# Local-global attention with a gated feed-forward on one core: every second head from the 17th on has its exponentials transposed in blocks by VectorE and placed by DMAs, queries load in pairs, and the planner has new due offsets

## The chip, the cores and the metric

The kernel runs on one core of one Trainium2 chip. The metric is the device time of one execution in microseconds (us), the median of several executions. A core has five engines that run their own instruction lists side by side: TensorE (PE) for matrix products, VectorE (DVE), ScalarE (ACT), GpSimd (POOL), and SyncE (SP), which here only issues DMAs. They meet through semaphores. SBUF is the on-chip memory, PSUM the memory that PE writes its products to.

## What is computed

```python
def _attn_ref(q_l, k_l, v_l, q_g, k_g, v_g):      # 8 batches, 8 heads, 512 local + 32 global positions, 64 wide
    s_g = scale * np.matmul(q_g, k_all.transpose(0, 1, 3, 2))
    out_g = np.matmul(sm(s_g), v_all)
    s_ll = scale * np.matmul(q_l, k_l.transpose(0, 1, 3, 2))
    mask = np.abs(pos[:, None] - pos[None, :]) <= window          # window = 32
    s_ll = np.where(mask, s_ll, -1000000000.0)
    s_lg = scale * np.matmul(q_l, k_g.transpose(0, 1, 3, 2))
    a_l = sm(np.concatenate([s_lg, s_ll], axis=-1))
    out_l = np.matmul(a_l, np.concatenate([v_g, v_l], axis=2))
...
def _moe_ref(x, w1, w2, w3, w_out):                # 4352 tokens, 512 -> 1024 -> 512
    a = x @ w1
    b = x @ w2
    h = a * b @ w3
    return (h @ w_out).astype(np.float32)
```

`sm` is a softmax over the last axis. A local query sees the 32 global keys and the local keys at most 32 places away; a global query sees all 544 keys.

## The kernel before

**Heads.** There are 64 heads (8 batches of 8). For each head n the 512 queries are four blocks e of 128. `scores` multiplies a block with the 192 or 256 keys that it can see (with the 32 global ones), into PSUM tile `s`. `minus_max` (VectorE) adds the mask, takes the row's extreme and writes the shifted scores to the SBUF buffer `P`, of which there are two, for even and for odd heads. `exps` (ScalarE) takes the exponential in place and sums rows. The next product needs these weights with the keys on the partitions, so `transposes` lets PE transpose `P` through an identity matrix: seven 128x128 pieces into PSUM tiles `t` (lines 391 and 394). `weights_hi` and `weights_lo` split what comes out into a rounded half and a remainder (fp32r pairs, so that two fast products give fp32 accuracy), into the single buffers `PTh` and `PTl` (local keys) and `G` (global keys). Five pieces e = 0, 1, 2, 3, 6 of that split come from the transposed head, two (4, 5) from the global queries. `values` then makes the head's output `av`; `values_half`, `values_sum`, `join` and `normalize` bring it to tile `u`, and `convert` splits it into the feed-forward's input `x`.

**Feed-forward.** w3 and w_out are multiplied once into w34 (`fold`, 64 products, PE line 692). For each half batch (256 tokens, and once for the global tokens) there are four quarters: `first` makes `ap` and `bp` (48 products of 256 columns, lines 555 to 557), `gate_a`/`gate_b`/`gate_hi`/`gate_lo` multiply and split them, `second` adds them into `acc` (12 products of 512 columns, lines 585 to 587). The weights arrive packed in 64-bit words and are unpacked by VectorE and ScalarE (`unit`, lines 612 to 616) while the first heads run.

**Order.** Nothing is ordered at run time. `list_schedule` takes every step with its engines, its cost (`COST`, ns) and a due time, and emits each engine's instructions in a fixed order: at each moment an engine takes, among the steps that are ready, the one with the lowest due time. A PE step that has become ready less than 600 ns ago ranks 6.0 us later, once the plan is past 250 us (`MARGIN`, `LATE`, `MAIN`). The due time is a natural one (a head every 8 us, then every 11.2 us) plus offsets from the tables `DUE` (by kind of step and by stage: stage 0 to 2 reach to about head 14, stage 3 is all that follows), `HEADS`, `UNITS` and `SUMS`. All DMAs are issued by SP, also in that fixed order; one that waits holds all behind it. `take` sets how many buffers a tile has, and so which later step waits for which earlier one.

Of the kernel before, what the change touches and what calls it, by code (L numbers as in the profile page):

```python
# [20 lines left out]
KD = 608  # L21
WIN = [(0, 192), (96, 256), (256, 256), (416, 192)]
PAT = [0, 192, 448, 704]
PW = 896
# [6 lines left out]
def i(ap):  # L31
# [3 lines left out]
NX, NO, NK, MA = (5, 6), 3, 3, 4  # L35
# [8 lines left out]
    w12l=((691, 1300), (420, 752)), w34h=587, w34l=681, scores=897, transposes=690, values=560, gscores=505,  # L44
# [26 lines left out]
    av=(0, -8.3, -53.5, 0), cb=(0, -42.6, 22.6, 0), cg=(-24.3, 42.6, 2.5, 0), clear=(36.2, 0, 0, 0),  # L71
    eg=(11.2, -14.5, 60.9, 0), exps=(-77.6, 1.9, 61.5, 0), fetch=(-6.1, 67.6, -28.7, 0), first0=(0, 0, -0.5, 0),
    first1=(0, 0, 14.2, 0), fold=(0, 82.7, 0, 0), ga=(0, 0, 19.2, 0), gb=(0, 0, -4.6, 0), gh=(0, 0, -57.6, 0),
    gl=(0, 0, -25.9, 0), gw=(0, 35.2, 8.4, 0), hi0=(0, 9.7, -58.6, 0), hi1=(0, -25.8, -77.7, 0),
    hi2=(0, -54.5, -10.4, 0), hi3=(0, -77.2, -22, 0), hi4=(0, -21.9, 24.2, 0), hi5=(0, -3.2, -31.3, 0),
    hi6=(0, 14, 6.1, 0), inv=(-41, -86.6, -72.2, 0), invi=(-2.4, 7.2, -63.4, 0), invo=(-5.2, -59.2, 61.1, 0),
    join=(0, -72, 8.5, 0), joing=(0, 41.8, -10.6, 0), kh=(-29, -66.2, 23.9, 0), kl=(25, -37.7, 45.9, 0),
    kph=(-76.1, 18.5, 3.8, 0), kpl=(22.5, 58.7, 76.8, 0), lcs=(-13.6, 0, 0, 0), lk=(10.3, -26.8, -37.4, 0),
    lkp=(6.7, -0.4, 59.5, 0), lo0=(0, -27.3, -31.1, 0), lo1=(0, -41.7, -128.1, 0), lo2=(0, -80.3, -32.8, 0),
    lo3=(0, -22.1, -19.6, 0), lo4=(0, -11.9, 72.6, 0), lo5=(0, 15.6, 35.1, 0), lo6=(0, -109, -94.1, 0),  # L80
    lq=(9.1, -81.9, -50.8, 0), lqg=(34.3, 46.7, 4.5, 0), lv=(22.9, 41.7, 72.5, 0), lvg=(-24.1, 73.7, -106.8, 0),
    mg=(11.1, 4.8, 28.3, 0), mmax=(-67.6, -19.9, 10.3, 0), mul=(0, 2.8, -12.7, 0), ng=(-9.8, -40.4, 19.2, 0),
    out=(0, 0, 31.5, 0), qgh=(-9.8, 6, 147.2, 0), qgl=(36.9, -10.2, 1.5, 0), qh=(54.2, -4.8, 102.4, 0),
    ql=(-40, 112.7, 18.6, 0), s=(173.8, 31.8, -49.9, 0), second=(0, 0, -11.5, 0), sg=(-103.1, 12.4, -39.4, 0),
    store=(0, 0, 68.3, 0), sum=(0, -31.9, 18.7, 0), t=(0, -40.4, -94.3, 0), tg=(0, -106.1, 15.3, 0),
# [17 lines left out]
}  # L103
SUMS = (-30.2, -40.9, -14, 28.4, 21.4, -13.3, 36.6, 38.3)
# [81 lines left out]
def band_attention_glu_kernel(  # L186
# [91 lines left out]
    def load_vg(b):  # L278
        vgr = p2.tile([64, 512], F32, tag="qr", name=f"vgr{b}", bufs=3)
# [36 lines left out]
    def prep_q(n, part, eng=None):  # L316
        if part == 0:
            T["qs", n] = p1.tile([128, 512], F32R, tag="qs", name=f"qs{n}")
            hi_of(T["qs", n][0:64], T["qr", n], eng)
        else:  # L320
            qs = T["qs", n]
            lo_of(qs[64:128], T.pop(("qr", n)), qs[0:64], eng)
# [827 lines left out]
```

## Time and profile before

| | |
|---|---|
| median of 3 runs | 900.78 us (899.81 to 900.85) |
| span of the profiled execution, first to last instruction | 896.8 us |
| what lies around the span, against the median | 4.0 us |
| VectorE busy | 631.9 us |
| ScalarE busy | 631.4 us |
| GpSimd busy | 424.1 us |
| DMA traffic | 87.06 MB |

The profile shows one execution. Its page names for each engine the busy time; a chain of waits that is followed back from the last instruction, which tells what the end hung on; groups of equal instructions with the mean duration of one; and DMA issues with the time until they have landed. The trace behind it answers for stretches of the span (windows) and as a list in order of time. Matrix products overlap each other in PE's pipeline: a listed duration of 0.28 us does not mean that the next one starts 0.28 us later. What one costs PE is the distance from start to start.

### The profile page before, as it was taken

To read this page: it belongs to the slowest core of one execution; us is meant where nothing else is said; L and a number is where in the kernel's file an instruction comes from. 1 tells how busy PE (TensorE), PEld (TensorE's weight loads), DVE (VectorE), ACT (ScalarE), POOL (GpSimd) and SP (SyncE) were. 2 spreads that over 40 slices of the span, in tenths; PEclk is the share of its full clock that TensorE was granted. 3 is DMA by queue.
4 is the path that set the end of the run, shared out by engine and by line. 5 is a ranking of instruction groups with operands and counts; after the bars stand their busy time and mean duration, and the time that the engine had idled before them with its cause. 6 is when DMAs were issued, how large, how long until landed. Compare 5 with 4: busy or idle time off the path is not lost.

```text
span 896.8 us, 17972 instructions
## 1 busy us (share of the span) xinstructions
PE 844.0 (94%) x6016; PEld 766.0 (85%) x6016; DVE 631.9 (70%) x1644; ACT 631.4 (70%) x1724; POOL 424.1 (47%) x492
## 2 busy tenths in 40 slices
PE   3879969799999999999999999999999999999995
PEld 2545549699899999999999999999999999999994
DVE  4998988778877778777777777777777787512111
ACT  5887887787878787878787878787877777512111
POOL 4454765655655555555555455555555545200000
PEclk9999989999999999999999999999999999999998
DMA  9877545332242423232323332323232311000000
GB/s 273 246 219 215 181 149 139 118 98 83 65 118 69 111 63 115 61 106 68 113 67 106 77 101 80 101 68 114 65 107 65 108 57 48 13 24 24 1 24 24
DMA packets 52853, 87.06 MB, mean 97 GB/s; under 512 B 16024, under 2 KB 17048, under 8 KB 52760
## 3 DMA queue, kind: packets, MB, share of 16 engines
q1 hardware_dynamic: 52760, 85.92, 33.1%
q8 instruction: 47, 0.77, 0.4%
q14 instruction: 46, 0.38, 0.2%
HBM read 76.84 MB, written 9.04 MB: 96 GB/s over the span
## 4 chain that ended last, share of the span: by engine, by line
PE 87%; DVE 4%; ACT 4%; DMA 2%; issue 1%; POOL 1%; SPq 1%; DVEq 0%; ACTq 0%; POOLq 0%
PE ap L555 7%; PE acc L585 7%; PE acc L587 7%; PE bp L555 7%; PE ap L556 7%; PE acc L586 7%; PE ap L557 7%; PE bp L556 7%; PE bp L557 7%; PE s L355 6%; PE av L446 6%; PE w L692 4%; PE t L391 3%; PE t L394 2%; PE av L441 2%; PE sg L482 2%
## 5 line engine op out<-in xcount | busy, mean ns | idle before, releaser
L555 PE MATMUL bp<-x,w12h 128*128 128x256 f32 x544 | 154.8, 285 | 0.8 <-DVE g__1696 L565 0.8
L555 PE MATMUL ap<-x,w12h 128*128 128x256 f32 x544 | 153.7, 283 | 0.0
L556 PE MATMUL ap<-x,w12h 128*128 128x256 f32 x544 | 152.1, 280 | 0.0
L557 PE MATMUL ap<-x,w12l 128*128 128x256 f32 x544 | 151.6, 279 | 0.0
L556 PE MATMUL bp<-x,w12h 128*128 128x256 f32 x544 | 151.2, 278 | 0.0
L557 PE MATMUL bp<-x,w12l 128*128 128x256 f32 x544 | 151.1, 278 | 0.0
L289 POOL TENSOR_TENSOR kl<-kr,kh 128x608 fp32r<-128x608 f32 x62 | 93.5, 1508 | 104.8 <-ACT kh L286 102.0
L363 ACT ACTIVATE P<-P,mn 128x192 f32<-128x192 f32 (+1 forms) x256 | 121.5, 477 | 5.5 <-DVE mn L359 4.8
L460 DVE TENSOR_TENSOR u<-av,cb 64x352 f32<-64x352 f32 x128 | 65.8, 521 | 58.5 <-ACT cb L286 55.8
L555 PEld LDWEIGHTS bp<-x,w12h 128*128 128x128 f32 x544 | 102.5, 188 | 1.9 <-DVE g__1696 L565 0.9
L556 PEld LDWEIGHTS ap<-x,w12h 128*128 128x128 f32 x544 | 103.6, 190 | 0.5
L555 PEld LDWEIGHTS ap<-x,w12h 128*128 128x128 f32 x544 | 103.5, 190 | 0.5
L556 PEld LDWEIGHTS bp<-x,w12h 128*128 128x128 f32 x544 | 102.5, 188 | 1.1
L557 PEld LDWEIGHTS ap<-x,w12l 128*128 128x128 f32 x544 | 103.4, 190 | 0.0
L557 PEld LDWEIGHTS bp<-x,w12l 128*128 128x128 f32 x544 | 102.4, 188 | 0.0
L359 DVE CUSTOM_DVE_ANT_0 P<-s,cs 128x192 f32<-128x192 f32 (+1 forms) x256 | 87.3, 387 | 7.7 <-PE s L355 5.6
L289 DVE TENSOR_TENSOR PTl<-t,PTh 32x96 fp32r<-32x96 f32 (+1 forms) x192 | 76.3, 397 | 19.2 <-ACT PTh L286 14.3
L286 ACT CAST PTh<-t 32x96 fp32r<-32x96 f32 (+1 forms) x190 | 66.5, 350 | 22.9 <-PE t L391 15.5
L286 ACT COPY cb<-av 64x352 f32<-64x352 f32 x128 | 57.0, 446 | 32.4 <-PE av L446 29.3
L355 PE MATMUL s<-kh,qs 128*128 128x192 f32 (+1 forms) x256 | 65.9, 292 | 8.5 <-DVE mg L497 3.3
L692 PE MATMUL w<-wo,w3f 128*128 128x512 f32 x128 | 63.8, 635 | 3.9 <-DVE wo L616 3.8
L446 PE MATMUL av<-PTl,vs 128*128 128x192 f32 (+1 forms) x256 | 64.5, 277 | 0.0
(786 smaller groups left out, 2350.8 us busy)
## 6 DMA issues: line engine op xcount, KB each, us to landing
kr<-in_kd_t_dram SPq DMA_DIRECT2D x128, 152.0 KB, 2.9
raw_w<-in_w_t_dram SPq DMA_DIRECT2D x24, 512.0 KB, 4.3
kpr<-in_kp_t_dram SPq DMA_DIRECT2D x32, 272.0 KB, 2.7
out_dram<-o SPq DMA_DIRECT2D x34, 256.0 KB, 2.2
qr<-in_q_t_dram SPq DMA_DIRECT2D x64, 128.0 KB, 2.7
vr<-in_v_t_dram SPq DMA_DIRECT2D x32, 256.0 KB, 2.7
R<-rd SPq DMA_DIRECT2D x64, 128.0 KB, 3.0
raw_wo<-in_wo_t_dram SPq DMA_DIRECT2D x8, 512.0 KB, 6.4
```

What stands on the lines that cost most here:

```text
L286: (nc.scalar.copy if eng in (None, nc.scalar) else eng.tensor_copy)(dst, src)
L289: (eng or nc.gpsimd).tensor_sub(dst, src, f(hi))
L355: nc.tensor.matmul(st[:, e, 0:w], qs[:, 128 * e : 128 * e + 128], kk[:, o : o + w], start=(j == e % 2 == 0), stop=(j == 1), skip_group_che ...
L359: nc.vector.tensor_tensor_reduce(blk(n, e), T["st", n][:, e, 0 : WIN[e][1]], masks[e], -0.125, 3.0e38, ALU.add, ALU.min, T["mn", n][:, e : ...
L363: nc.scalar.activation(blk(n, e), blk(n, e), AF.Exp, bias=T["mn", n][:, e : e + 1], scale=-1.0, accum_out=T["sm", n][:, e : e + 1])
L446: nc.tensor.matmul(av[:, o : o + c1 - c0], v, pt[:, j, c0:c1], start=False, stop=(j % 2 == y == 1), skip_group_check=True)
L460: nc.vector.tensor_add(T["u", n // 2][r : r + 64, x], T.pop(("av", n, x))[r : r + 64, 0:352], T["cb", n][r : r + 64, x])
L555: nc.tensor.matmul(d, wh[:, k, c, :], x[:, 0, 0:w], start=(k == m % 2 == 0), stop=False, skip_group_check=True)
L556: nc.tensor.matmul(d, wh[:, k, c, :], x[:, 1, 0:w], start=False, stop=False, skip_group_check=True)
L557: nc.tensor.matmul(d, wl[:, k, c, :], x[:, 0, 0:w], start=False, stop=(k == 3), skip_group_check=True)
L585: nc.tensor.matmul(a, gh[:, m % 2, sl], wh, start=(m == 0), stop=False)
L692: nc.tensor.matmul(T["w34", t], T["w3f", t, j // 4][:, j % 4], T["wo"][:, j], start=(j == 0), stop=(j == 7))
```

## The change

From head 17 on, every odd head ("turned", 24 heads) is no longer transposed by PE. `minus_max` writes its shifted scores to another layout of `P` (1120 instead of 896 columns): eight slots of four blocks e of 32 columns. `turn` lets VectorE transpose 32x32 blocks in place with three instructions (5 slots = 640 columns, 2 slots = 256, 32 columns). A 32x32 transpose leaves each block at its old place in the partitions, so DMAs move the blocks: `turned_out` writes five slots to a DRAM buffer `pd` with four DMAs (rows of 512 bytes) and copies two pieces of 32x96 from partition group to partition group; `turned_in` reads `pd` back into `P` in the new arrangement with two DMAs. The split into halves then reads `P` in SBUF instead of `t` in PSUM, in four pieces instead of five, and its remainders (`lo`) may run on GpSimd as well as on VectorE. These heads have their scores due 6 us earlier (`AHEAD`). The queries of two heads load with one DMA of 128 partitions; the split of an odd head's query works on the upper half. GpSimd clears a spare part of both `P` once. The four tables of offsets are new throughout: those of before lie within about 185 us of zero, and those of stage 3 were all zero; the new ones reach to 2900 us, in stage 3 too.

```diff
-PW = 896
+PW = 1120
+TURN, FROM, AHEAD = 2, 16, 6.0
+def turned(n):
+    return n >= FROM and n % TURN == TURN - 1
...
-    av=(0, -8.3, -53.5, 0), cb=(0, -42.6, 22.6, 0), cg=(-24.3, 42.6, 2.5, 0), clear=(36.2, 0, 0, 0),
+    T=(0, 0, 0, -189.6), av=(0, -2661.5, -798.8, -1384), av_=(0, 0, 0, -1664), cb=(0, -875.8, -862.7, -832.2),
...
-    def load_q(n):
-        b, h = divmod(n, H)
-        qr = p2.tile([64, 512], F32, tag="qr", name=f"qr{n}", bufs=3)
-        nc.sync.dma_start(qr, q_t[b, h])
+    def load_q(m):
+        b, p = divmod(m, NP)
+        qr = p2.tile([128, 512], F32, tag="qr", name=f"qr{m}", bufs=NQ)
+        nc.sync.dma_start(qr, q_t[b, 2 * p : 2 * p + 2].rearrange("h d s -> (h d) s"))
...
+    def turn(n):
+        g = grid(n)
+        nc.vector.transpose(g[:, 1:6], g[:, 1:6])
+        nc.vector.transpose(g[:, 0:8:7], g[:, 0:8:7])
+        nc.vector.transpose(g[:, 1, 0], g[:, 6, 0])
+
+    def turned_out(n):
+        P = Ps[n % 2]
+        d = T["pd", n] = dram.tile([5, 32, 4, 128], F32, tag="pd", name=f"pd{n}", bufs=2)
+        for x in range(4):
+            nc.sync.dma_start(d[:, :, x].rearrange("s p w -> p s w"),
+                              P[32 * x : 32 * x + 32, 128:768].rearrange("p (s w) -> p s w", s=5))
+        nc.sync.dma_start(P[96:128, 32:128], P[0:32, 32:128])
+        nc.sync.dma_start(P[0:32, 1024:1120], P[96:128, 896:992])
+
+    def turned_in(n):
+        P = Ps[n % 2]
+        d = T.pop(("pd", n))
+        nc.sync.dma_start(P[:, 256:768], d[1:5].rearrange("s p x w -> (s p) (x w)"))
+        nc.sync.dma_start(spread(n, [256]), d[0].rearrange("p (a b) w -> p a (b w)", b=2))
...
+        if turned(n):
+            t -= 4.0 + AHEAD
+            take("pd", 2, ("pd", n), ("dw", n))
+            add(("T", n), only("DVE", COST["turn"]), t, [("exps", n, e) for e in range(4)], turn, n)
+            add(("dw", n), dma(6), t + 1.0, [("T", n)], turned_out, n, nbytes=360448)
+            add(("dr", n), dma(2), t + 2.0, [("dw", n)], turned_in, n, nbytes=327680)
```

What this makes of the instruction lists is seen at head 39, in the middle of the program. **PE** before, where the products `bp` of a quarter end, head 39 is transposed (`t_39`) and head 40's scores `s` begin:

```order
L555 MATMUL bp_1_4_6646<-x_3_1_5532,w12h_1472 128x256
L556 MATMUL bp_1_4_6646<-x_3_1_5532,w12h_1472 128x256
L557 MATMUL bp_1_4_6646<-x_3_1_5532,w12l_1473 128x256
L391 MATMUL t_39_6737<-cs,P_74 128x128 x4
L394 MATMUL t_39_6738<-cs,P_74 128x128 x3
L355 MATMUL s_6748<-kh_6634,qs_6639 128x192
L355 MATMUL s_6748<-kl_6662,qs_6639 128x192
```

and PE now, at the same place:

```order
L627 MATMUL bp_1_4_6672<-x_3_1_5588,w12h_1192 128x256
L628 MATMUL bp_1_4_6672<-x_3_1_5588,w12h_1192 128x256
L629 MATMUL bp_1_4_6672<-x_3_1_5588,w12l_1193 128x256
L395 MATMUL s_6692<-kh_6563,qs_6609 128x192
L395 MATMUL s_6692<-kl_6583,qs_6609 128x192
```

The seven transposes are gone, and the scores follow the feed-forward directly; over the program PE has 280 of these transposes instead of 448, and all its other products are as many as before. **VectorE** now, at head 39 (`P_74`): three block transposes, then the inverse of its row sums (`sm`) and work of head 38 (`u`) and of the feed-forward (`gl`):

```order
L429 STREAM_TRANSPOSE P_74<-P_74 128x640
L430 STREAM_TRANSPOSE P_74<-P_74 128x2x128
L431 STREAM_TRANSPOSE P_74<-P_74 128x32
L408 TENSOR_SCALAR sm_6525<-sm_6525 128x4
L409 RECIPROCAL sm_6525<-sm_6525 128x4
L532 TENSOR_TENSOR u_6645<-av_38_6615,cb_6634 64x352
L532 TENSOR_TENSOR u_6645<-av_38_6621,cb_6634 64x352
L311 TENSOR_TENSOR gl__6668<-g__6607,gh__6664 128x512
```

The first remainder of head 39 (`PTl<-P_74`) stands 20 rows further on, behind a gate, a global softmax and the four `minus_max` of head 40. Before, the remainders (`PTl<-t_39`, `G<-t_39`) were read from PSUM and there was no such gap. **SP** now, with the same head's DMAs (`pd` is the DRAM buffer, `rd` and `R` carry its row sums, `kr` and `qr` are loads of later heads):

```order
L279 DMA kr_6604<-in_kd_t_dram 64x608
L280 DMA kr_6604<-in_kd_t_dram 64x608
L437 DMA pd_6627<-P_74 32x5x128 x4
L439 DMA P_74<-P_74 32x96
L440 DMA P_74<-P_74 32x96
L414 DMA rd_6670<-sm_6525 128x4
L445 DMA P_74<-pd_6627 128x512
L446 DMA P_74<-pd_6627 32x2x256
L420 DMA R_6559<-rd_6670 64x512
L273 DMA qr_6738<-in_q_t_dram 128x512
```

Eight DMAs are new in a turned head; the last two wait until the first six have landed, and the loads behind them wait as well.

More of the change, by code (lines that the diff above doesn't have):

```diff
@@ L43 @@
     gl=(691, 1295), out=587, shift=(434, 295), scale=(680, 440), merge=(676, 424), w12h=(676, 423),
-    w12l=((691, 1300), (420, 752)), w34h=587, w34l=681, scores=897, transposes=690, values=560, gscores=505,
+    w12l=((691, 1300), (420, 752)), w34h=587, w34l=681, scores=897, turn=1260, turned=((620, 512, 691, 1295), (290, 96, 257, 290), (290, 96, 257, 290), (620, 512, 691, 1295)),
+    transposes=690, values=560, gscores=505,
     gtrans=465, first=1440, second=1405, fold=900,
@@ L76 @@
[L76 to L85, printed above, removed]
@@ L318, in prep_q @@
             T["qs", n] = p1.tile([128, 512], F32R, tag="qs", name=f"qs{n}")
[L319 to L322 removed]
+        qs, r = T["qs", n], 64 * (n % 2)
+        qr = T["qr", n // 2][r : r + 64]
+        if part == 0:
+            hi_of(qs[r : r + 64], qr, eng)
+        else:
+            lo_of(qs[64 - r : 128 - r], qr, qs[r : r + 64], eng)
     def prep_v(n, s, part, eng=None):
@@ L340, in prep_kp, with grid, spread, cut @@
             lo_of(T["kpl", m], T.pop(("kpr", m)), T["kph", m], eng)
+    def grid(n):
+        return Ps[n % 2][:, 0:1024].rearrange("p (s e q) -> p s e q", e=4, q=32)
+    def spread(n, dims):
+        P = Ps[n % 2]
+        steps = [1]
+        for w in dims[:0:-1]:
+            steps.insert(0, steps[0] * w)
+        return bass.AP(P.tensor, P.offset, [[PW, 32], [768, 2], *([x, w] for x, w in zip(steps, dims))])
+    def cut(n, ap):
+        return ap.rearrange("p (s q) -> p s q", q=32) if turned(n) else ap
     def blk(n, e):
-        return Ps[n % 2][:, PAT[e] : PAT[e] + WIN[e][1]]
+        if not turned(n):
+            return Ps[n % 2][:, PAT[e] : PAT[e] + WIN[e][1]]
+        s = 0 if e else 2
+        return grid(n)[:, s : s + WIN[e][1] // 32, e]
     def scores(n):
@@ L719, in moved @@
             kind += str(key[2])
+        if k in BY_HEAD and turned(key[1]):
+            kind += "_"
         d = DUE.get(kind, (0, 0, 0, 0))[stage]
@@ L768, in tile_orders @@
             take("kr", NK, (*k, "r"), ("load", *k))
-        for k in (("q", 0), ("q", 1), ("vg", 0)):
-            take("qr", 3, (*k, "r"), ("load", *k))
+        take("qr", NQ, ("q", 0, "r"), ("load", "q", 0))
+        take("kr", NK, ("vg", 0, "r"), ("load", "vg", 0))
         for k in (("sg", 0), ("s", 0), ("sg", 1), ("tg", 0)):
@@ L777, in tile_orders @@
                 take("kr", NK, ("k", n + 2, "r"), ("load", "k", n + 2))
-                take("qr", 3, ("q", n + 2, "r"), ("load", "q", n + 2))
+                if n % 2 == 0:
+                    take("qr", NQ, ("q", n // 2 + 1, "r"), ("load", "q", n // 2 + 1))
                 if (n + 2) % H == 0:
-                    take("qr", 3, ("vg", (n + 2) // H, "r"), ("load", "vg", (n + 2) // H))
-            for x in range(2):
+                    take("kr", NK, ("vg", (n + 2) // H, "r"), ("load", "vg", (n + 2) // H))
+            for x in range(2 * (not turned(n))):
                 take(f"t{x}", 1, (f"t{x}", n), ("t", n))
@@ L849, in head @@
             me = ("av", n, x)
-            add(me, only("PE", COST["values"]), t + 4.2 + 0.1 * x, [("lo", n, e) for e in range(7)] + v + [("av", n, 0)] * x, values, n, x)
+            add(me, only("PE", COST["values"]), t + 4.2 + 0.1 * x, [("lo", n, e) for e in parts] + v + [("av", n, 0)] * x, values, n, x)
             tiles["vs", n // 2].append(me)
@@ L1051, in band_attention_glu_kernel @@
     add(("load", "cs"), dma(1), -40.0, (), constants, nbytes=294912)
-    for x, (ap, ns) in enumerate(((QG, 525), (PTh, 957), (PTl, 962), (G[64:128], 552), (vgs[64:128], 952))):
-        k = ("QG", 0, 1, 2, "vgs")[x]
-        add(("clear", k), only("POOL", ns), (-60.0, -4.0, -4.0, -4.0, -4.0)[x], (), clear, ap)
+    spare = [p[:, 896:1024] for p in Ps]
+    for x, (ap, ns) in enumerate(((QG, 525), (PTh, 957), (PTl, 962), (G[64:128], 552), (vgs[64:128], 952), *((s, 200) for s in spare))):
+        k = ("QG", 0, 1, 2, "vgs", "P0", "P1")[x]
+        add(("clear", k), only("POOL", ns), (-60.0, -4.0, -4.0, -4.0, -4.0, -4.0, -4.0)[x], (), clear, ap)
     for n, u in enumerate(ORDER):
```

100 lines of the change are left out of this document (76 added, 24 removed), and 21 rows, old and new, of the table UNITS.

## The prediction

> **What bounds the kernel now.** I read the page's first lines and its chain of waits, then the windows, then PE's list in order of time.
>
> ```profile
> span 896.8 us, 17972 instructions
> PE 844.0 (94%) x6016; PEld 766.0 (85%) x6016; DVE 631.9 (70%) x1644; ACT 631.4 (70%) x1724; POOL 424.1 (47%) x492
> PE 87%; DVE 4%; ACT 4%; DMA 2%; issue 1%; POOL 1%; SPq 1%; DVEq 0%; ACTq 0%; POOLq 0%
> ```
>
> PE is busy for 94% of the span and carries 87% of the chain that sets the end. That is an average over stages, so the windows come next. Columns: stretch, its length, busy us (instructions) of PE, weight loads, VectorE, ScalarE, GpSimd, then granted clock, DMA share, GB/s.
>
> ```profile
> 0.00:40.00 40.00, 22.40 (x82) 14.14 (x82) 26.20 (x71) 26.90 (x67) 20.09 (x25) 0.96 0.88 257
> 40.00:80.00 40.00, 33.78 (x133) 19.34 (x134) 37.30 (x87) 32.14 (x88) 17.44 (x22) 0.96 0.80 227
> 80.00:160.00 80.00, 68.35 (x369) 50.72 (x368) 68.86 (x165) 65.44 (x174) 54.11 (x66) 0.94 0.54 162
> 200.00:300.00 100.00, 98.59 (x751) 93.56 (x751) 78.35 (x209) 78.76 (x221) 52.71 (x60) 1.00 0.31 89
> 408.71:500.56 91.85, 91.85 (x708) 87.50 (x708) 71.52 (x195) 73.12 (x205) 48.57 (x55) 1.00 0.31 88
> 760.00:880.00 120.00, 120.00 (x884) 113.14 (x884) 33.02 (x65) 29.10 (x66) 11.61 (x16) 1.00 0.05 16
> ```
>
> Three stages. In the ramp PE has gaps while VectorE (37.3 of 40) and ScalarE unpack weights. From about 200 us PE is full: the row from 408.71 to 500.56 is one period of eight heads, PE 100%, VectorE 78%, ScalarE 80%, DMA 31%. From 770 us only feed-forward is left, PE still full. So from 200 us on a microsecond less for PE is a microsecond less at the end, as long as nobody keeps PE waiting. The turned heads 17 to 63 lie almost wholly there.
>
> **What the change takes from PE.** The listed durations overlap, so I go by starts.
>
> ```profile
> 511.32 0.60 PE L391 MATMUL t<-cs,P 128*128 128x128 f32 x4
> 511.76 0.49 PE L394 MATMUL t<-cs,P 128*128 128x128 f32 x3
> 512.01 0.33 PE L355 MATMUL s<-kh,qs 128*128 128x192 f32 x1
> 512.98 0.30 PE L555 MATMUL ap<-x,w12h 128*128 128x256 f32 x1
> 515.74 0.28 PE L555 MATMUL bp<-x,w12h 128*128 128x256 f32 x1
> 517.68 0.40 PE L585 MATMUL acc<-w34h,gh__6974 128*128 128x512 f32 x1
> 519.07 0.28 PE L441 MATMUL av<-G,vgs 128*128 128x256 f32 x1
> ```
>
> The seven transposes hold PE from 511.32 to 512.01, **0.69 us** (by their listed mean of 278 ns it would be 1.95). 24 heads x 0.69 = **16.6 us** off PE. Its other products stay the same in number.
>
> **What it adds, and what hides it.**
>
> ```profile
> L289 DVE TENSOR_TENSOR PTl<-t,PTh 128x512 fp32r<-128x512 f32 x64 | 43.9, 687 | 8.5 <-ACT PTh L286 7.3
> L289 DVE TENSOR_TENSOR G<-t,G 32x384 fp32r<-32x384 f32 x64 | 35.8, 560 | 1.0
> L289 DVE TENSOR_TENSOR PTl<-t,PTh 32x96 fp32r<-32x96 f32 x128 | 32.3, 253 | 10.7 <-ACT PTh L286 7.0 <-ACT G L286 0.5
> L289 DVE TENSOR_TENSOR G<-t,G 32x128 fp32r<-32x128 f32 x64 | 17.9, 280 | 1.5 <-ACT G L286 0.5
> L289 DVE TENSOR_TENSOR qs<-qr,qs 64x512 fp32r<-64x512 f32 x23 | 27.4, 1189 | 1.6 <-ACT qs L286 0.8
> L289 POOL TENSOR_TENSOR qs<-qr,qs 64x512 fp32r<-64x512 f32 x41 | 55.7, 1359 | 13.4 <-ACT qs L286 6.4 <-issue 2.4 <-POOL kl L289 1.1
> L510 DVE TENSOR_SCALAR Pg<-Pg,smg 128x544 f32<-128x544 f32 x16 | 9.4, 584 | 0.6
> L612 DVE TENSOR_SCALAR raw_w12s<-raw_w12s 128x256 int32<-128x256 int32 x16 | 8.4, 529 | 1.7 <-DMA raw_w12s<-in_w_t_dram 1.6
> ```
>
> No row shows a block transpose. By the nearest one (584 ns for 544 columns) the 928 columns of three instructions cost 1.0 us; by the slowest near one (529 ns for 256) 1.9. I take 1.1, nearer the float row: 24 x 1.1 = 26 us for VectorE. [...] It loses the remainders from PSUM: 0.687 + 0.560 + 2 x 0.253 + 0.280 = 2.03 us a head, 48.8 in all. In the new order it does 29 large and 19 small remainders from SBUF: 19 x 0.253 plus 29 times between 0.687 and 1.189 (the row with two SBUF inputs), so 25 to 39 us. And 21 of the query remainders go to GpSimd: 25 us off VectorE, 28 onto GpSimd, which has half its time free. VectorE ends between +2 and -23 us: its cover at 78% stays. ScalarE's rounding reads as many elements as before.
>
> [...]
>
> **The new wait.** A turned head's weights now go through DRAM, and this chain must fit between its scores and its values on PE.
>
> ```profile
> L363 ACT ACTIVATE P<-P,mn 128x256 f32<-128x256 f32 x128 | 64.0, 502 | 0.2
> L363 ACT ACTIVATE P<-P,mn 128x192 f32<-128x192 f32 x128 | 57.9, 452 | 5.3 <-DVE mn L359 4.8
> L363 ACT ACTIVATION_READ_ACCUMULATOR P<-P,mn 128x1 f32 x256 | 48.4, 189 | 0.0
> L359 DVE CUSTOM_DVE_ANT_0 P<-s,cs 128x192 f32<-128x192 f32 x128 | 45.3, 354 | 6.9 <-PE s L355 5.6
> L286 ACT CAST PTh<-t 128x512 fp32r<-128x512 f32 x64 | 37.5, 586 | 16.1 <-PE t L391 15.5
> L286 ACT CAST PTh<-t 32x96 fp32r<-32x96 f32 x126 | 29.0, 230 | 6.8 <-PE t L394 4.1
> out_dram<-o SPq DMA_DIRECT2D x34, 256.0 KB, 2.2
> R<-rd SPq DMA_DIRECT2D x64, 128.0 KB, 3.0
> rd<-sm SPq DMA_DIRECT2D x64, 2.0 KB, 2.0
> q1 hardware_dynamic: 52760, 85.92, 33.1%
> 517.36 0.47 SPq L257 DMA_DIRECT2D kr<-in_kd_t_dram  x1
> 517.88 0.59 SPq L258 DMA_DIRECT2D kr<-in_kd_t_dram  x1
> ```
>
> First `minus_max` 0.35; four exponentials with their sums 2 x 0.691 + 2 x 0.641 = 2.66; block transposes 1.1; six writes, five issues at 0.47 to 0.59 and then 2.0 to 2.2 to land, 4.9; two reads, one issue and 3.0 to land, 3.5; rounding two large and two small pieces 1.63 and a last remainder, 2.1; handovers about 0.7, my estimate. Sum **15.3 us**. At worst: transposes 1.9, a last remainder under contention +0.5, and the write bound by its 704 packets: 0.331 x 16 x 896.8 / 52760 = 90 ns each, 704 / 16 x 0.09 = 4.0, with landing 6.2. Sum 17.9.
>
> The room for it: between head 39's scores and its values PE's order has 72 first products at (515.74 - 512.98) / 24 = 0.115, 24 second ones at (519.07 - 517.68) / 6 = 0.232, 16 scores at 0.121, 5 transposes at 0.099 and 14 others at about 0.115: **17.9 us**. The same count gives 19.6, 19.3 and 19.6 at heads 41, 43 and 45, and the pattern repeats every eight heads. So 2.6 us are spare at one turned head in four and 4 or more at three, for queueing on engines that are 80% busy. Behind the waiting reads SP holds `R`, `qr` and a key load; behind the waiting rounding ScalarE holds exponentials of the next head and a gate's rounding, for which PE's `t` and `acc` wait. I count the wait as hidden, with small slips:
>
> - **Slips, +4.** From head 15 on the new offsets are hundreds to thousands of us, so the planner's 6 us against steps that are only just ready no longer decides, and attention goes first the moment it is ready in the plan; any lateness then reaches PE. Before, that was so only early: in 200 to 300 us PE lost 1.41 of 100, later nothing. Over some 560 us that bounds it at 8; below it is 0. I take half.
> - **Ramp, +3.** Ahead of the first gate VectorE's order has eight more pieces of small w12 weights, each with a shift (529 ns) and a merge of about as much: 8 us more where it is 93% busy. But the big w12 pieces come earlier in ScalarE's order. Bounds -10 and +10.
> - **Tail, -1.4.** See the last gate:
>
> ```profile
> 882.33 0.70 DVE g__11784 L565
> 883.06 0.63 ACT gh__11786 L286
> 883.73 0.50 PE acc L585
> ```
>
> PE has 1.4 us of `acc` (six products) left to fill this gate of 1.4 us and its waits; the new order keeps twice as much for it. At most 1.4, at least 0.
>
> The 24 x 0.68 MB of new traffic come on a DMA share of 0.31; eight new issues of about 0.5 a turned head lie beside 22 us. The paired query loads save 32 issues that nobody waited for: 0.
>
> **Sum.** 896.8 - 16.6 + 4 + 3 - 1.4 = 885.8 us of span. Around the span lie 4.0 us (896.8 against the median of 900.8), so **889.8 us**.
>
> **The rivals.**
> - *The gain is kept whole and the ramp shortens.* No slips, ramp -7: 900.8 - 16.6 - 1.4 - 7 = 876; with the ramp unchanged 883. Middle 880. For it: PE has 35 us of gaps in the first 160. Against: VectorE limits there, and gets no lighter. 12%.
> - *The trip through DRAM is late at the tight heads only.* 1.3 us late (the packet bound) at six heads: 889.8 + 7.8 = 897.6. 10%.
> - *Given back in the new order.* Slips at 8, ramp at 10: 900.8 - 16.6 - 1.4 + 18 = 900.8. That is also where "PE is not the bound after all" would end. 10%.
> - *The trip through DRAM takes over as the bound.* Queueing eats the spare time, and write and transposes are at their bounds, 1.3 + 0.8 = 2.1 us late. Six heads lose 2.1, eighteen with 1.3 more room 0.8: 27 us. 900.8 - 16.6 + 27 - 1.4 + 3 = 912.8. It is slower from a lateness of 1.6 us on: 6 x 1.6 + 18 x 0.3 = 15, the net gain. [...] Against: both bounds at once, and no spare at all. 16%.
>
> That PE keeps its transposes is excluded by the order.
>
> **Chances and range.** Forecast 889.8 (884 to 895): 52%. Faster is forecast, whole gain and tight heads: 74%. Within 0.2%, about what a measurement of this kernel can tell from no change: 10%. Slower: 16%. The range of 879 to 903 takes in the forecast, the two middle rivals and most of the fastest, and leaves out the slowest.
>
> **What would show it.** PE at 100% in a period of eight heads that is 2.8 us shorter than 91.85; block transposes near 1.1 us together; `pd` landing within 5 us of its first issue; no waits of `av` or `acc` on ScalarE, GpSimd or DMA beyond 200 us; first full PE stretch again near 200 us. Wrong would be: PE waits at every turned head's `av`, VectorE over 90%, or a granted clock under 1.00 there.

## The result, and the profile after

| | before | after |
|---|---|---|
| median (runs) | 900.82 us (899.53 to 903.29, 6) | 895.14 us (893.53 to 898.31, 6) |
| profiled execution: span | 896.8 us | 896.5 us |
| ratio of times, 95% interval | | 0.9944 (0.9923 to 0.9964) |

The kernel became faster by 5.7 us by the medians (5.0 by the ratio, which is taken over all runs): inside the range, but at most about half of the forecast 11.0. The profiled execution was the slowest of its six (898.31 us), so its span hardly differs from before; a second profile of the same kernel (`again`, below) was of one that took 892.58 us. In every execution of this result and of the experiments the time is only 1.7 to 2.0 us longer than the span of the same execution. So the 4.0 us that were read as lying around the span before are in part something else: the profiled execution of before was a fast one, of about 898.6 us by this estimate (896.8 + 1.8). The forecast difference of 11.0 does not depend on that, and the two spans 896.8 and 890.8 compare about 898.6 with 892.58 us. The page's first lines after the change:

```profile
span 896.5 us, 17912 instructions
PE 832.8 (93%) x5848; PEld 753.6 (84%) x5848; DVE 630.3 (70%) x1623; ACT 616.4 (69%) x1671; POOL 491.2 (55%) x592
```

The windows after the change (stretch, length, busy us of PE, weight loads, VectorE, ScalarE, GpSimd, granted clock, DMA share, GB/s):

```profile
0.00:40.00 40.00, 19.13 (x61) 11.90 (x62) 24.33 (x63) 22.96 (x53) 15.70 (x22) 1.00 0.84 260
40.00:80.00 40.00, 35.79 (x139) 20.15 (x138) 34.38 (x83) 32.04 (x82) 15.54 (x22) 0.96 0.79 227
80.00:160.00 80.00, 58.98 (x251) 41.75 (x249) 64.21 (x159) 62.48 (x169) 51.03 (x59) 0.81 0.50 153
160.00:200.00 40.00, 39.54 (x306) 37.81 (x307) 35.72 (x92) 33.79 (x95) 26.47 (x33) 1.00 0.34 97
200.00:300.00 100.00, 97.26 (x740) 91.88 (x739) 78.48 (x222) 78.93 (x226) 64.65 (x77) 1.00 0.42 113
400.00:500.00 100.00, 99.17 (x751) 93.88 (x750) 77.04 (x208) 77.07 (x215) 65.84 (x78) 1.00 0.46 119
500.00:600.00 100.00, 98.20 (x742) 92.89 (x741) 75.21 (x208) 76.31 (x213) 66.84 (x78) 1.00 0.45 119
700.00:760.00 60.00, 58.01 (x444) 54.99 (x443) 48.78 (x125) 44.77 (x131) 34.01 (x44) 1.00 0.35 91
```

Two things stand out. PE is no longer full everywhere beyond 200 us. And the stretch 80 to 160 us, where PE was busy for 68.35 us at a clock of 0.94, now has 58.98 at 0.81; PE is full from 160 us instead of 200, which returns 5.6 of these 9.4 us. This row is of before:

```profile
160.00:200.00 40.00, 33.94 (x235) 31.83 (x234) 29.50 (x82) 30.84 (x89) 25.33 (x32) 0.91 0.33 103
```

The dip sits in 30 us; the first row is of before, the second of after:

```profile
120.00:150.00 30.00, 21.29 (x147) 20.38 (x148) 24.90 (x62) 24.93 (x71) 20.36 (x23) 0.83 0.45 125
```

```profile
120.00:150.00 30.00, 13.47 (x62) 11.50 (x61) 24.42 (x64) 24.50 (x69) 17.78 (x22) 0.67 0.46 132
```

The rows also say what is missing there. Before, the first product of the feed-forward (`ap`) starts at 132.5 us, and 86 of the 147 products between 120 and 150 us are `ap` and `bp`. After, the first one starts at 151.4 us (150.3 in `again`), so that in the dip PE has only attention, whose products wait for other engines.

**What PE lost, as one number.** Busy time can't be compared between clocks (up to 200 us a product of 256 columns takes PE 0.213 us where the records show the clock at 0.5, and 0.114 at 1.00), so I sum for each profile what every distance between the starts of two neighbouring matmuls has beyond the median distance behind a matmul of that line and shape. That counts gaps and half clock alike. "Head" is the start of the first matmul plus the sum up to 200 us, "main" the sum from 200 to 760, "tail" what follows. (The expectations below give the loss before 200 us without the start of the first matmul, so their figures are 9 to 11 us lower.)

| profile | span | head | main | tail | ideal PE work |
|---|---|---|---|---|---|
| before | 896.8 | 61.5 | 5.0 | 1.0 | 819.2 |
| after | 896.5 | 70.1 | 15.4 | 0.2 | 800.8 |
| after, again | 890.8 | 69.0 | 10.8 | -0.1 | 801.0 |

The last column is the sum of the median distances: what they make of the span without any loss. What starts with the last matmul takes 10.2 us more, the same in all three. With it, ideal + head + main + tail is the span to about 0.1 us, so the loss can be placed: from before to `again` it is -18.2 + 7.5 + 5.8 - 1.1 = -6.0. Some two fifths of the gain are lost in the head. Of the 7.5 us there, 5.3 are idle time of PE, as the first 200 us show (before, then `again`: 41.5 us idle, then 46.8); the other 2.2 are products that follow each other more slowly.

```profile
0.00:200.00 200.00, 158.47 (x815) 116.03 (x816) 161.87 (x402) 155.32 (x414) 116.97 (x143) 0.94 0.62 182
0.00:200.00 200.00, 153.21 (x763) 111.64 (x764) 158.95 (x395) 151.85 (x396) 110.25 (x134) 0.90 0.60 178
```

**Where the main part loses.** PE's waits between 200 and 800 us (engine, line, what it waited for, us in total, times, longest), first the only one of before, then the longest of the profile after:

```profile
PE s L355 <- DVE TGg L527: 1.3, 1, 1.3
```

```profile
PE sg L554 <- DVE mn L399: 3.7, 3, 2.0
PE ap L627 <- ACT as__2970 L633: 1.1, 1, 1.1
PE s L395 <- ACT TGg L599: 0.9, 1, 0.9
PE av L518 <- DVE PTl L311: 0.9, 1, 0.9
PE av L513 <- DVE G L311: 0.6, 1, 0.6
```

The longest wait is not at `av`, which uses the turned weights, but at `sg`, the global scores. The chain of waits shows how (start, us, what):

```profile
698.73 0.38 SPq L414
...
699.27 0.32 SPq L445
699.59 0.05 issue
699.65 7.03 DMA P<-pd
...
706.76 0.62 ACT PTh L308
...
708.02 0.42 DVE P L399
...
708.78 0.77 PE sg L554 x4
```

The read-back (L445), which SP issues behind the row sums' write (L414), takes 7.03 us here; only then does ScalarE round `PTh` out of `P` and VectorE take the remainder. This is head 57. What waits behind it is `minus_max` (L399) of head 58, an even head, which writes the other `P`. VectorE's list shows why:

```profile
702.19 0.41 DVE L399 CUSTOM_DVE_ANT_0 P<-s,cs 128x256 f32<-128x256 f32 x1
702.53 0.07 DVE L399 DVE_READ_ACCUMULATOR2_ANT mn<- 128x1 f32 x1
707.41 0.69 DVE L311 TENSOR_TENSOR PTl<-P,PTh 128x512 fp32r<-128x512 f32 x1 [4.80 <-ACT PTh L308]
708.02 0.42 DVE L399 CUSTOM_DVE_ANT_0 P<-s,cs 128x256 f32<-128x256 f32 x1
```

Two of head 58's four `minus_max` are done at 702.6 us; head 57's remainder comes next in VectorE's fixed order, waits for 4.80 us, and the other two stand behind it. `minus_max` is what empties PSUM tile `s`, and the global scores `sg` take turns with it in that one buffer. So here a late trip reaches PE through VectorE's list, and not through the values. Heads 25, 33, 41 and 49 have the same order, the remainder between the second and the third `minus_max` of the next head, and PE's three waits at `sg` stand behind heads 33, 41 and 57. At head 39, which was looked at before, the remainder stands behind all four.

ScalarE's own wait and the DMAs' medians:

```profile
ACT PTh L308 <- DMA P<-pd: 24.6, 17, 3.5
```

```profile
pd<-P SPq DMA_DIRECT2D x96, 80.0 KB, 1.9
P<-pd SPq DMA_DIRECT2D x24, 256.0 KB, 4.5
P<-pd SPq DMA_DIRECT2D x24, 64.0 KB, 4.4
```

The trip is late for ScalarE at 17 of 24 heads. The writes do as forecast (from the end of the block transposes to the last landing 4.4 us in the median, for a forecast of 4.9), the reads do not: 4.5 us instead of 3.0.

### The profile page after: what moved, and what is told of

Read it like the earlier page. It is cut to its first block, busy times and chain, and to the rows that moved or that the text cites. A ratio compares the mean times of both kernels' runs of the same rounds, so it can differ in the third digit from the quotient of the medians.

```text
span 896.5 us, 17912 instructions
## 1 busy us (share of the span) xinstructions
PE 832.8 (93%) x5848; PEld 753.6 (84%) x5848; DVE 630.3 (70%) x1623; ACT 616.4 (69%) x1671; POOL 491.2 (55%) x592
## 3 DMA queue, kind: packets, MB, share of 16 engines
q1 hardware_dynamic: 76824, 102.24, 40.8%
## 5 line engine op out<-in xcount | busy, mean ns | idle before, releaser
L311 POOL TENSOR_TENSOR qs<-qr,qs 64x512 fp32r<-64x512 f32 x62 | 82.2, 1325 | 83.1 <-ACT qs L308 68.7
L627 PEld LDWEIGHTS ap<-x,w12h 128*128 128x128 f32 x544 | 102.5, 188 | 4.1 <-ACT as__2970 L633 1.5
L628 PEld LDWEIGHTS ap<-x,w12h 128*128 128x128 f32 x544 | 102.3, 188 | 1.3 <-POOL x L311 0.2
L399 DVE CUSTOM_DVE_ANT_0 P<-s,cs 128x192 f32<-128x192 f32 (+1 forms) x256 | 86.9, 387 | 13.1 <-PE s L395 11.0
L311 POOL TENSOR_TENSOR kl<-kr,kh 128x608 fp32r<-128x608 f32 x49 | 74.8, 1526 | 12.6 <-ACT kh L308 9.4
L764 PE MATMUL w<-wo,w3f 128*128 128x512 f32 x128 | 63.7, 645 | 10.8 <-DVE w3f L688 10.8
L395 PEld LDWEIGHTS s<-kh,qs 128*128 128x128 f32 x256 | 51.2, 200 | 22.4 <-DVE mg L569 8.8
```

Source lines behind the costliest of these rows:

```text
L311: (eng or nc.gpsimd).tensor_sub(dst, src, f(hi))
L395: nc.tensor.matmul(st[:, e, 0:w], qs[:, 128 * e : 128 * e + 128], kk[:, o : o + w], start=(j == e % 2 == 0), stop=(j == 1), skip_group_che ...
L399: nc.vector.tensor_tensor_reduce(blk(n, e), cut(n, T["st", n][:, e, 0 : WIN[e][1]]), cut(n, masks[e]), -0.125, 3.0e38, ALU.add, ALU.min, T ...
L627: nc.tensor.matmul(d, wh[:, k, c, :], x[:, 0, 0:w], start=(k == m % 2 == 0), stop=False, skip_group_check=True)
L628: nc.tensor.matmul(d, wh[:, k, c, :], x[:, 1, 0:w], start=False, stop=False, skip_group_check=True)
L764: nc.tensor.matmul(T["w34", t], T["w3f", t, j // 4][:, j % 4], T["wo"][:, j], start=(j == 0), stop=(j == 7))
```

## The experiments

All times are medians; ratios are against runs of before on the same chip, whose median lay between 898.5 and 900.0. Times of different experiments can come from different chips, and 1.5 us between them then say little.

### Is it the trip that the main part loses by?

**again**: the changed kernel once more, as a base.

> The changed kernel once more, beside the others on one chip. Its profiled execution was one of the slowest of its six (898.3 of 893.5 to 898.3 us). If the spread comes from the landing of the read-back of `pd` (median 4.7 us from issue of the first read to landing of the second, longest 7.4), a profile of a median execution shows fewer or shorter late landings and fewer gaps on PE between 200 and 760 us (7.4 us of idle PE there in the first profile). If the spread comes from the ramp, the gaps before 200 us change instead (46.6 us of idle PE there). Time: 893 to 898.

Measured 894.74 us, ratio 0.9946 (0.9930 to 0.9963). Main is 10.8 and PE's waits at `sg` are 1.2 us, where the first profile had 15.4 and 3.7; ScalarE's wait for the read is 16.1 us in 14 times instead of 24.6 in 17. The trip's lateness scatters from one execution to the next.

**told_read**: the planner is told that the reads take longer.

```diff
-add(("dr", n), dma(2), t + 2.0, [("dw", n)], turned_in, n, nbytes=327680)
+add(("dr", n), dma(2), t + 2.0, [("dw", n)], turned_in, n, nbytes=327680 + 260000)
```

> The planner is told 1.0 us more for the read-back, about what the trace shows (4.7 us against the 4.0 that it counted); nothing else. The ramp is planned before the first such read, so it stays the same. Theory A (the gaps of the main phase come from the read-back landing later than planned): they fall from 7 us to 3 or less, and the time by 4 to 6 us, to about 889 to 891. Theory B (they come from an order that puts attention first the moment it is ready, whatever it waits for): the gaps stay at 5 to 10 us and the time within 2 us of the changed kernel.

Measured 913.23 us, ratio 1.0157 (1.0135 to 1.0180): both theories missed. Main is 29.4, and PE now waits at the values and at `acc`; its first rows are:

```profile
PE av L513 <- DVE G L311: 4.4, 4, 2.2
PE acc L657 <- ACT gh__9669 L308: 1.7, 1, 1.7
PE acc L657 <- ACT gh__6933 L308: 1.7, 1, 1.7
```

One microsecond more in one cost makes another plan of the whole program, and the due offsets do not fit it. The experiments that follow on the trip keep the planned order, but for old_tables, and change only what a step emits.

**read_input**: the two reads fetch the same number of bytes from `q_t`, which was never written.

```diff
-nc.sync.dma_start(P[:, 256:768], d[1:5].rearrange("s p x w -> (s p) (x w)"))
+nc.sync.dma_start(P[:, 256:768], q_t[b, h - 1 : h + 1].rearrange("h d s -> (h d) s"))
...
```

> The two reads of a turned head fetch as many bytes in the same rows from the queries in DRAM instead of the buffer `pd` that was just written; the writes stay, and so does the order, so the weights of the turned heads are not the right ones. If the read-back is slow because it reads what has just been written, it lands in 3.0 to 3.5 us instead of 4.7, nearly no wait for it is left on ScalarE (24.6 us in the changed kernel), and by theory A the main phase loses 4 to 7 us of gaps: 888 to 891. If it is slow for its shape or for traffic, it still lands in 4.5 and the time is that of the changed kernel.

Measured 894.5 us, ratio 0.9948 (0.9932 to 0.9964), and the reads land in 4.5 and 4.4 us as before. That they read what was just written is not what makes them slow. What does stays open: in the profile after, a query load (`qr`) of as many bytes in rows of as many lands in 3.5 us.

**old_tables**: the changed kernel with the due offsets of before.

> The turned heads and the paired queries with the offset tables of before (kinds with a new name get none). If the new tables cost the ramp its 9 us (PE starts lost beyond their usual distance before 200 us: 60.0 us against 50.6), they come back. If the new order's lack of a margin costs the main phase, its gaps fall as well, since stage 3 has no offsets then and the 6 us rule decides again. Both: 900.8 - 16.6 and little given back, 883 to 888. If instead the trip through DRAM needs the new order to fit, PE waits at the turned heads' values and the time is 895 or more.

Measured 925.26 us, ratio 1.0293 (1.0272 to 1.0314). Main is 43.2, and PE waits at the values (19.5 us in two rows):

```profile
PE av L499 <- DVE G L297: 10.2, 9, 2.6
PE av L499 <- POOL G L297: 9.3, 3, 4.5
```

With the old offsets the trip is not hidden: old_noturn (below), with these offsets and no turned head, has a main of 6.8. The head is 70.5 with the old offsets too, so its loss does not come from the new offsets alone.

**no_trip**: the same order, but the kernel leaves out the writes and the reads of the trip (and clears all of the spare part of `P` instead, columns 896 to 1120).

```diff
 def turned_out(n):
-    ...
+    pass
 def turned_in(n):
-    ...
+    pass
```

> The planned order stays that of after to the instruction, but the six writes and two reads of each turned head are not issued, so that its hi/lo operations follow the block transposes at once (the weights of the turned heads are then not the reference's). Theory A (the late read-back holds P, the row maxima and the score tile, which is what TensorE waits for at the global scores): TensorE's loss between 200 and 760 us falls from 10.8 to about 5 us, the loss before 200 us stays near 60, and the time falls by 5 to 6 us to 888.5-890. Theory B (the gaps after 200 us belong to the new order whatever the trip does): loss there stays at 9-12 us, time within 1.5 us of 894.7. The ramp is no question here.

Measured 889.24 us (887.60 to 889.61), ratio 0.9884 (0.9867 to 0.9902). Main falls to 6.6, as theory A has it for the part played by the trip, and the trip costs 894.74 - 889.24 = **5.5 us** (5.6 by the ratios; the intervals do not overlap). No wait at `sg` is left. This profile also gives a clean period of eight heads, from head 32's first score to head 40's:

```profile
406.60:495.88 89.28, 89.28 (x680) 84.89 (x680) 71.21 (x187) 70.14 (x197) 61.70 (x73) 1.00 0.33 91
```

It is 91.85 - 89.28 = 2.57 us shorter than before, for four turned heads: 0.64 us each. In `again` the same period, with the trip, takes 89.37.

**own_tiles**: the same order and the same trip, but the reads land in two tiles of the outputs' ring instead of `P`. The two small pieces that are copied within `P` are still read from there, so `P` is freed only in part.

```diff
-nc.sync.dma_start(P[:, 256:768], d[1:5].rearrange("s p x w -> (s p) (x w)"))
-nc.sync.dma_start(spread(n, [256]), d[0].rearrange("p (a b) w -> p a (b w)", b=2))
+R, E = T["tR", n] = [p2.tile([128, 512], F32, tag="o", name=f"t{c}{n}", bufs=NO) for c in "RE"]
+nc.sync.dma_start(R, d[1:5].rearrange("s p x w -> (s p) (x w)"))
+nc.sync.dma_start(E[0:32], d[0].rearrange("p x w -> p (x w)"))
...
```

> The planned order of after, to the instruction; only the two reads of a turned head now land in two tiles of the outputs' ring instead of back in P, and the hi/lo operations read them there. The trip is as long as before, but P is free once the writes have left it. Theory A (what is lost is P held until the late hi/lo operations): loss between 200 and 760 us falls from 10.8-15.4 to 6-8 us, close to the 6.6 without any trip, and the time falls from 894.7 to 890-892. Theory A' (the late hi/lo operations themselves, or the engines' order behind them, hold PE): no change, 893.5-896. If the ring of the outputs is too tight, waits appear at acc and the time is above 897.

Measured 892.59 us (891.42 to 896.65), ratio 0.9932 (0.9912 to 0.9952). The interval overlaps that of `again`, so the time decides nothing. In the profile PE still waits at `sg`, once, for 0.9 us (1.2 in `again`), and ScalarE waits for the read a little less than the 16.1 us of `again`:

```profile
ACT PTh L308 <- DMA tR<-pd: 13.1, 11, 2.4
```

Main is 10.1, above the 6 to 8 expected and hardly under the 10.8 of `again`. That the held `P` is the way to PE, as theory A has it, is not borne out. The result fits the chain above: own_tiles leaves VectorE's list as it was, and the remainder still stands ahead of the next head's `minus_max`. No run moves the remainder behind them, so how much of the 5.5 us goes this way is open.

### Where does the head lose?

| kernel | head | main | time, us | ratio to before (95%) |
|---|---|---|---|---|
| before | 61.5 | 5.0 | 898.5 to 900.0 | |
| clears_only | 62.3 | 4.8 | 899.67 | 1.0002 (0.9990 to 1.0014) |
| vg_only | 76.8 | 10.3 | 923.88 | 1.0282 (1.0262 to 1.0302) |
| pairs_only | 69.6 | 12.6 | 914.80 | 1.0179 (1.0158 to 1.0199) |
| old_noturn | 69.0 | 6.8 | 907.81 | 1.0099 (1.0079 to 1.0119) |
| new_noturn | 71.2 | 11.0 | 912.44 | 1.0137 (1.0115 to 1.0160) |
| hybrid | 82.1 | 40.8 | 935.21 | 1.0395 (1.0374 to 1.0415) |
| pairs_old_order | 68.0 | 5.0 | 903.00 | 1.0028 (1.0016 to 1.0040) |
| own_tiles | 70.4 | 10.1 | 892.59 | 0.9932 (0.9912 to 0.9952) |
| old_ramp_150 | 76.1 | 10.3 | 899.14 | 0.9989 (0.9975 to 1.0003) |
| old_ramp_190 | 68.6 | 9.1 | 890.86 | 0.9892 (0.9873 to 0.9911) |
| old_ramp_205 | 63.3 | 14.6 | 890.11 | 0.9905 (0.9880 to 0.9929) |
| old_ramp_215 | 62.8 | 14.8 | 892.03 | 0.9916 (0.9897 to 0.9935) |
| old_ramp_225 | 63.5 | 12.7 | 890.07 | 0.9901 (0.9873 to 0.9929) |

**old_noturn** and **new_noturn**: no turned heads (`FROM = 64` instead of 16), with the old and with the new due offsets. What is left of the change is the pairing, the global values in the keys' ring, the wider `P` and the two clears.

> The due times of before and no turned heads at all: what is left of the change is the queries in pairs, the global values in the ring of the keys, the wider P buffers and two more clears. Theory C (these structural edits cost the ramp): loss before 200 us is near 60 instead of 50.6 and the time is 8-11 us above before, 908-912. Theory D (the ramp of after is bought by its tables or the turned heads): loss before 200 us is 50-53, and the time is within 2 us of 900.

> The new due times without turned heads: transposes are back on TensorE in all heads. By theories C and D the loss before 200 us is near 60 as in after (same tables, same structure). The 18.2 us of TensorE work come back: 894.7 + 18 = 913 if the later part loses as little as after, more (up to 930) if the stage-3 due times fit only a plan with turned heads.

Both heads are near 70, whatever the offsets. So the head's loss is there without any turned head. That fits theory C, but does not yet say whether the edits themselves or the plan made of them costs it.

**hybrid**: turned heads and new stage-3 offsets behind the old offsets of the first stages.

> Turned heads and the stage-3 due times of after, but the due times of the first three stages, of the first twelve heads and of the weight units are those of before. By theory C the loss before 200 us stays near 60 (as with all old tables: 60.7), by theory D it falls to about 51, and with the later part as in after (11-15 us) the time is then near 885; by C it is 893-900. If the later part is planned anew because the earlier one ends otherwise, its loss goes up to 20-40 us and the time beyond 900, and only the ramp's number counts.

The head got worse than with either set whole (82.1), and the later part fell apart as well (40.8). It says only that the tables do not mix.

**clears_only**, **vg_only**, **pairs_only**: the kernel before with one of the edits each, planned anew with its own offsets.

```diff
 clears_only
 ...
-(vgs[64:128], 952))):
+(vgs[64:128], 952), (xg[:, 0], 200), (xg[:, 1], 200))):
 ...
 vg_only
-vgr = p2.tile([64, 512], F32, tag="qr", name=f"vgr{b}", bufs=3)
+vgr = p2.tile([128, KD], F32, tag="kr", name=f"vgr{b}", bufs=NK)[0:64, 0:512]
 ...
 pairs_only
-qr = p2.tile([64, 512], F32, tag="qr", name=f"qr{n}", bufs=3)
-nc.sync.dma_start(qr, q_t[b, h])
+qr = p2.tile([128, 512], F32, tag="qr", name=f"qr{m}", bufs=2)
+nc.sync.dma_start(qr, q_t[b, 2 * p : 2 * p + 2].rearrange("h d s -> (h d) s"))
 ...
```

> The kernel before with nothing but two more clears of 128 columns on GpSimd in the ramp (of columns of xg that are written later), planned with the tables of before. Theory C1 (the queries in pairs cost the ramp): loss before 200 us stays at 50-52, time 899-901. Theory C2 (the ramp's plan is a fit to one exact set of steps, and any change of it costs): the loss before 200 us moves by several us, time 903-910.

> The kernel before with nothing but the global values moved from the ring of the queries to the ring of the keys, planned with the tables of before. C1: loss before 200 us 50-53, time 899-902. C2: the loss before 200 us moves by several us, time 903-910. If the fuller ring of the keys is the price (C4), it shows as in after: near 59 and 907.

> The kernel before with nothing but the queries loaded in pairs into a ring of two (the global values in a tile of their own), planned with the tables of before. C1: loss before 200 us about 59 as with all the structural edits together, time 907-909. C2: several us like the other two, 903-910, of no particular size. C4: as before, 899-901.

The clears cost nothing. The ring alone costs 25 us and the pairs alone 16, while old_noturn, with both, costs 8. Prices that shrink when they are added are hardly prices of the edits themselves. Each edit makes another plan, and the runs fit the reading that it decides how well the offsets suit that plan. Theory C1 (the pairs, with 8 us of their own) falls; C2 has the direction right for two of the three, but both lie beyond its 903 to 910 us. For the pairs the next run separates the edit from the plan; for the ring no such run was made.

**pairs_old_order**: pairs in the order of before, to the instruction; the load of an even head brings both, that of an odd head is not issued.

```diff
+if n % 2 == 0:
+    qr = p2.tile([128, 512], F32, tag="qr", name=f"qr{n}", bufs=2)
+    nc.sync.dma_start(qr, q_t[b, h : h + 2].rearrange("h d s -> (h d) s"))
...
```

> The kernel before in its own planned order, to the instruction; only the load of an even head brings the queries of its pair and that of an odd head is not issued (the global values have a tile of their own). The planner does not know of it. If the cost of the pairs is physical (the larger transfer lands later, the ring of two holds loads back), the loss before 200 us goes to 57-60 and the time to 907-915 as in pairs_only. If it comes from planning anew with due times that were fitted to another set of steps, the loss stays at 50-52 and the time at 898-901.

Measured 903.00 us in 12 runs, 0.28% (3.0 us) above before: between the two theories. The pairs cost some 3 us in the head even where the order stays (the profiled execution took 904.94 us, so its head of 68.0 is on the high side); the other 13 us of pairs_only are the new plan.

**old_ramp_150, _190, _205, _215, _225**: own_tiles with the order of before, engines included, up to 150, 190, 205, 215 or 225 us of the plan, and the order of after behind it (the first global values stand in the outputs' ring there).

```diff
-for _, n, e in list_schedule(steps, after, held):
+for _, n, e in planned(steps, after):   # a list: 782 to 1191 steps of before, then the rest as in after
...
```

> own_tiles with the planned order of before for the first 1003 steps (what before plans up to 190 us, engines included; queries in pairs, the first global values in the outputs' ring), and then the order of after for all other steps. If the ramp's loss is a matter of the order alone, the loss before 200 us falls from 60.7 to 51-53, the rest stays as in own_tiles (10), and the time falls from 892.6 to 883-885, the best of all. If the paired queries or the fuller rings cost the ramp whatever the order, the loss stays at 57-61 and the time at 890-893. If the seam costs, the loss between 200 and 300 us rises by some us.

> As old_ramp_190 with the seam at 150 us of the plan (782 steps of before). In the order of before the long gaps lie at 120-195 us (TensorE was full only from 195), in that of after at 120-155: with the seam at 150 the loss before 200 us should be 51-57 and the time 883-889 by the theory of order, 890-893 by the physical one.

> As old_ramp_190 with the seam at 225 us of the plan (1191 steps of before). The loss before 200 us is then 51-52 by the theory of order, as in old_ramp_190; the first turned head (transposed near 240 us) has less room behind the seam, so up to 3 us more there: 883-887. By the physical theory 890-893.

> As old_ramp_225 with the seam at 205 us of the plan (1088 steps of before). The gaps of 1.9 and 0.9 us that stand behind the seam at 225 should go, with the loss before 200 us still at 51-56: 886-889 us. If they only move with the seam, 890.

> As old_ramp_205 with the seam at 215 us (1141 steps of before): 886-889 us if the seam's gaps shrink, 890 if they only move.

With the seam at 205 us or later the head is back at 62.8 to 63.5, 7 us below own_tiles and 2 above before, with turned heads, pairs and rings all in place. With the seam at 190 us it is still 68.6, where the expectation's 51 to 53 is some 62 on this scale. With the seam at 225 us PE's busy time in the dip is nearly that of before (21.29), though the clock stays low, and the first `ap` starts at 133.4 us; first own_tiles, then old_ramp_225:

```profile
120.00:150.00 30.00, 13.31 (x63) 10.72 (x61) 25.23 (x65) 25.15 (x71) 18.70 (x23) 0.74 0.49 144
```

```profile
120.00:150.00 30.00, 20.58 (x126) 19.54 (x127) 22.52 (x59) 23.42 (x67) 20.59 (x23) 0.77 0.45 129
```

In these three, 2.6 to 4.7 us come back behind the seam as loss in the main part, and the time is 0.6 to 2.5 us below own_tiles, not the 8 of the expectation; the intervals of the ratios overlap that of own_tiles. A seam at 150 lies inside the dip and makes it worse. That the order makes most of the head's loss is shown; that the better head can be had together with the better main part is not. The fastest complete versions are old_ramp_190, _205 and _225, at 890.1 to 890.9 us and ratios of 0.989 to 0.991, which do not differ clear of noise: some 4 us under the changed kernel.

## Why the forecast was right in its direction and half wrong in its size

Against the second profile of after, whose count closes at -6.0 us:

| term | forecast | measured | from |
|---|---|---|---|
| transposes off PE | -16.6 | -15.4 | 24 x 0.64, the period in no_trip |
| head ("ramp") | +3 | +7.5 | head 69.0 against 61.5 |
| slips | +4 | +3.0 | main 10.8 against 5.0 is 5.8; 2.8 of it are taken off because the sum of medians says -18.2 for the transposes and the period -15.4 |
| tail | -1.4 | -1.1 | tail |
| sum | -11.0 | -6.0 | |

- **The failed step is the ramp term.** The prediction said that the first part is planned anew, but it sized that by eight more pieces of small weights on VectorE: +3, with bounds of ±10. It measured +7.5. The eight pieces are there (11 instead of 3 ahead of the first gate), yet VectorE did not become the limit: up to 160 us its rows add up to 122.9 us busy, where before they add up to 132.4. What the runs show in its place is the order itself: the feed-forward starts 18 to 19 us later and leaves PE without other work in the dip, and with the order of before up to 205 us or later the head is back at 62.8 to 63.5. The paired loads, costed at 0, cost about 3 us at fixed order.
- **Transposes: right.** 0.64 us a head for 0.69, and the period is 2.57 us shorter for the forecast 2.8.
- **Block transposes: right.** They last 840, 402 and 168 ns, 1.41 in sum, inside the bounds of 1.0 to 1.9; from the start of the first to the end of the last it is 1.26.
- **VectorE's net: above the range.** 631.9 before, 630.3 after. The forecast's own terms (26 - 48.8 + 25 to 39 - 25) add up to -9 to -23, not to +2 to -23 as it says. The block transposes took 33.8 us instead of 26. The new remainders took 40.4; at the prices from PSUM, 29 large and 19 small ones would be 24.7. So they came 15.7 us dearer, above the forecast's 25 to 39 as well, but not where that range looked, at large ones of up to 1189 ns: the large remainders took 781 and 718 ns for 687, the small ones 970 for 253. The trace of after shows what the small ones stand beside: 18 of the 19 begin while GpSimd is in a remainder that also reads two tiles in SBUF, and they end 0.11 to 0.12 us behind it, whether they began 0.06 or 1.1 us after it; the nineteenth began before its GpSimd neighbour and took 0.235 us. The forecast's +0.5 for a last remainder "under contention" is the difference of two rows of before, 1189 and 687 ns, which name no cause. GpSimd itself took 67 us more than before.

```profile
L311 DVE TENSOR_TENSOR PTl<-P,PTh 128x512 fp32r<-128x512 f32 x18 | 14.1, 781 | 28.1 <-ACT PTh L308 28.1
L311 DVE TENSOR_TENSOR G<-P,G 32x512 fp32r<-32x512 f32 x11 | 7.9, 718 | 0.6 <-ACT G L308 0.3
L311 DVE TENSOR_TENSOR PTl<-P,PTh 32x96 fp32r<-32x96 f32 x19 | 18.4, 970 | 6.0 <-ACT PTh L308 4.7 <-DMA vgr<-in_vg_t_dram 1.1
```

- **The trip: "hidden" was wrong, and the slips' size came out near by luck.** The +4 was laid to attention going first in the plan. no_trip has that order and loses 6.6, near the 5.0 of before; the rest is the trip, 4.2 us between these two profiles and 5.5 between the medians. The read was sized from `R<-rd` (3.0 us to land, 3.5 with its issue); from the first read's issue to the second's landing it takes 4.7. The room was counted rightly (head 39's values start 18.0 us after its last score, for 17.9 forecast), but the way to the last remainder was not: its sum was 15.3 us, with 0.7 for handovers that was the author's estimate and worked out from no row, and in `again` it takes 17.0 at head 39 and 20.4 at head 41. From head 19 to 61 only 0.1 to 1.7 us are left to the values, where 2.6 and 4 or more were counted. It takes 17.0 at head 39 in no_trip too, so there it is the order of the engines' lists and not the trip. And the prediction looked for what waits on ScalarE and SP; it did not look at what stands behind the remainder on VectorE, the next head's `minus_max`.
- **Rivals.** "Given back in the new order" came in half: a head near its bound of 10, without slips of 8. The trip as the bound did not come: PE waits at `av` for 1.5 us in two times after 200 us. The trip late at the tight heads only is near in kind: PE waits at `sg` three times, for 3.7 us in all, 1.2 in `again`.
- **What would show it.** The period and the landing of the writes came as said, the clock is 1.00 in every window from 200 to 880 us. The block transposes took 1.41 us for the "near 1.1". The first full PE stretch came 40 us earlier than said and yet with more lost.

## What to carry to other kernels

Where a table of due times fits one exact set of steps, cost every edit as a new plan: price the edit itself by a run with the edit and the old order, and do not cost a regrouped load at 0 unseen. When a result takes a longer way round, look at what stands behind its first reader in that engine's list, at every position of the pattern and not at one: here half of the next head's `minus_max` stood there, at one turned head in four. And look at what an engine has to fill its gaps with: the dip came where the feed-forward started later.

## What was not expected of the hardware

- A read of 256 KB in rows of 2 KB landed 4.2 to 4.5 us after its issue in the median (4.5 in after, 4.2 in `again`, 4.5 in read_input), whether the data were just written or never. At head 39 of the profile after it was issued at 498.55 us. The last packet on record ahead of it ended at 499.06, and its own first one began at 500.73; the first sixteen packets took 0.55 to 0.98 us and later ones 0.084, and it had landed by 502.94. Half the time passed before the first packet, 1.67 us of it with no packet on record.
- In the profile after the packets of 512 bytes took about 30 ns each, a third of the 90 that the forecast's bound came from.
- In the ramp the products of 256 columns follow each other every 0.213 us where the records show the clock at 0.5, and every 0.114 at 1.00. Up to 200 us they show it below 0.9 for 23.9 us before, 34.1 and 41.0 in the two profiles of after, and 23.9 in old_ramp_225, whose order is that of before. But the head does not simply follow that time: own_tiles and old_ramp_205 both have 30.7 us of it, with heads of 70.4 and 63.3.
